# Linear attention ahead of two mixture layers: the exponentials of a chunk one step later in a hand-written pipeline

## Chip, cores and metric

The kernel runs on one core of a Trainium2 chip. The metric is device time in microseconds (us), the median of several runs. The engines are named as the profile names them: PE (TensorE, its matmuls), PEld (its weight loads), DVE (VectorE), ACT (ScalarE), POOL (GpSimd) and SP (SyncE, which here only issues transfers). Each engine runs its own instructions strictly in program order.

## What is computed

Three parts follow each other: attention with random features, a gated layer and a layer that mixes eight experts. Only the first is touched.

```python
def phi(x):                      # x: q or k, scaled by 64 ** -0.25
    proj = einsum('bhsd,md->bhsm', x, omega)
    h = proj - sum(x * x, -1) / 2
    return exp(h - max(h, -1)) / sqrt(m)
kv  = einsum('bhsm,bhsd->bhmd', phi(k), v);  z = sum(phi(k), 2)
out = (phi(q) @ kv) / (phi(q) @ z + 1e-6)    # batch 4, heads 8, 576 positions, width 64, 128 features
x = moe2(moe(out))
```

## The kernel before

The attention cuts q and k into 36 chunks of 128 partitions by 512 numbers (eight groups of 64). Chunk 0 and chunk 17 hold the tails of k, 18 and 35 those of q; the rest alternate, k on odd and q on even numbers. A pipeline that is written out by hand goes through them in steps. The list ORDER (L63) says which stage is issued in which place of a step, and for which chunk: a pair (name, n) works on chunk step - n. So the order of the list is the order of each engine's queue, and n is how many steps after its own number a chunk reaches a stage. The stages are:

- load and loadv (L442, L453), on SP's queue: x two steps ahead, v one step ahead, ahead of all else in the step.
- s0 (L467): squares of x on POOL into one buffer, and two foldings there, from 64 to 16 per group (chunk 0 takes the square on ACT and is not folded). s0r (L482) sums them on DVE, s0n (L487) scales the sums on POOL.
- s2p (L494): the projection, 16 small matmuls on PE into one of two double banks of PSUM. s2m (L511): maximum of it on DVE. s2b and s2c (L515, L521): the bias of the exponentials, two small DVE operations. s2x (L525): the exponentials, 8 on ACT, four each in two places.
- s3 (L531): for k the product with v into a bank of the ring "nu" (banks 1 and 2), for q transposes into the ring of banks 0 and 3. s3a (L552): ACT copies them out.
- s4 (L565): for q the product with kv, in two halves into the two banks of "nu". s4d, s4r, s4n (L581 to L600): the denominators, their reciprocals and the quotient on DVE. s5 (L602): transposes of that, into banks 0 and 3. s5a on ACT and s5b on DVE (L618, L623): the result as a rounded part xh and a rest xl.
- pump (L629): one piece of work on the weights of the next layer (conversions on ACT, DVE and POOL).

Chunk i is projected in step i + 1. After 38 steps the first matmuls of the next layer (moe1, next(m1) at L662) are issued between the last stages, and the rings change to banks that these leave free (DRAIN, L646).

In a step of before, DVE's queue is in this order: s5b, s2m, s0r, s2b, s4d, s2c, the rest of s4, pump. ACT's is s5a, s3a, s2x, pump, with one pump between the halves of s2x. So xl of a step stands ahead of its maximum, and the exponentials belong to the chunk whose maximum was taken in the same step.

Of the kernel before, what the change touches and what calls it, by code (L numbers as in the profile page):

```python
# [11 lines left out]
F32 = mybir.dt.float32  # L12
F32R = mybir.dt.float32r
AF = mybir.ActivationFunctionType
ALU = mybir.AluOpType
AX = mybir.AxisListType
# [4 lines left out]
P = 128  # L21
B, H, S, D = 4, 8, 576, 64
# [12 lines left out]
SCALE = float(D) ** -0.25  # L35
# [15 lines left out]
class Kernel:  # L51
    def __init__(self, tc, x, v, vt, omega, wg, wv, wo, w2g, w1, w2, out):
# [7 lines left out]

    ORDER = [("s5a", 7), ("s3a0", 4), ("s2p", 1), ("s5b", 7), ("s2m", 1), ("s40", 5), ("s0r", 0), ("s3a1", 4),  # L63
             ("s2b", 1), ("s4d0", 5), ("s2c", 1), ("s0", -1), ("s30", 3), ("s31", 3), ("s2x0", 1), ("s41", 5),
             ("s0n", 0), ("pump", 3), ("s5", 6), ("s2x1", 1), ("s4d1", 5), ("s4r", 5), ("s4n0", 5), ("s4n1", 5),
             ("pump", 4)]
    RINGS = dict(tr3=(0, 3), tr5=(0, 3), nu=(1, 2), a=(0, 1, 2, 3), b=(4, 5, 6, 7))

    DRAIN = dict(RINGS, tr3=(4, 5), tr5=(6, 4, 5), nu=(7, 6))


    EARLY = 1

# [322 lines left out]
    def attention(self, m1):  # L398
        tc, nc = self.tc, self.nc
        if True:  # L400
            af, ident = self.af, self.ident
            t0 = af.tile([P, 4, 512], F32, tag="t0", name="at0")
            t1 = af.tile([P, 2, 1024], F32, tag="t1", name="at1")
            t2 = af.tile([P, 4, 512], F32, tag="t2", name="at2")
# [3 lines left out]
            sm = af  # L408
# [27 lines left out]
            NCH = len(chunks)  # L436
# [5 lines left out]
            def load(i):  # L442
                side, bp, hp, j = chunks[i]
                c = st[i]
                n = 8 if hp is None else 2 * hp + j
                k = turn("x", 3)
                xt = c["xt"] = xts[turn("xt", 4)]
                c["x"] = t0[:, k].rearrange("p (a d) -> p a d", d=D)
                for w, t in ((0, t0[:, k]), (1, xt)):
                    nc.sync.dma_start(t, self.x["qk".index(side), w, bp, n])  # L450
                c["idx"] = (lambda a, h: 2 * a + h) if hp is None else (lambda a, h: 4 * h + a)

            def loadv(i):  # L453
                side, bp, hp, j = chunks[i]
                c = st[i]
                if side == "q":
                    return
                if hp is None:
                    c["vz"] = vzts[2 * bp:2 * bp + 2]
                    for j in range(2):  # L460
                        nc.sync.dma_start(c["vz"][j].rearrange("p a d -> p (a d)"), self.vt[bp, j])
                else:
                    z = c["vz"] = vz[nvz[0] % NVZ]
                    nvz[0] += 1
                    nc.sync.dma_start(z.rearrange("p a d -> p (a d)"), self.v[bp, 2 * hp + j])

            def s0(i):  # L467
                c = st[i]
                sqv = c["x"]
                if i < self.EARLY:  # L470
                    c["xx"] = t2[:, i].rearrange("p (a d) -> p a d", d=D)
                    c["ssq"] = sm.tile([P, 8], F32, tag="ssq", name=f"ssq{i}", bufs=4)
                    nc.scalar.activation(c["xx"], sqv, AF.Square)
                    return
                xx = t0[:, 3].rearrange("p (a d) -> p a d", d=D)
                nc.gpsimd.tensor_tensor(xx, sqv, sqv, op=ALU.mult)
                ssq = sm.tile([P, 8], F32, tag="ssq", name=f"ssq{i}", bufs=4)
                nc.gpsimd.tensor_tensor(xx[:, :, 0:32], xx[:, :, 0:32], xx[:, :, 32:64], op=ALU.add)
                nc.gpsimd.tensor_tensor(xx[:, :, 0:16], xx[:, :, 0:16], xx[:, :, 16:32], op=ALU.add)
                c["xx"], c["ssq"] = xx, ssq  # L480

            def s0r(i):  # L482
                c = st[i]
                xx = c["xx"] if i < self.EARLY else c["xx"][:, :, 0:16]
                nc.vector.tensor_reduce(c["ssq"], xx, axis=AX.X, op=ALU.add)

            def s0n(i):  # L487
                c = st[i]
                nsq = sm.tile([P, 8], F32, tag="nsq", name=f"nsq{i}", bufs=4)
                eng = nc.vector if i < self.EARLY else nc.gpsimd  # L490
                eng.tensor_scalar(nsq, c["ssq"], -SCALE * SCALE / 2, None, op0=ALU.mult)
                c["nsq"] = nsq

            def s2p(i):  # L494
                side, bp, hp, j = chunks[i]
# [132 lines left out]

            pump = lambda i: self.attn_pump()  # L629
            fns = dict(s0=s0, s0r=s0r, s0n=s0n, s2p=s2p, s2m=s2m, s2b=s2b, s2c=s2c, s4r=s4r, s5=s5, s5a=s5a, s5b=s5b, pump=pump)  # L630
            halves = dict(s2x=s2x, s3=s3, s3a=s3a, s4=s4, s4d=s4d, s4n=s4n)

            def stage(n):
                if n in fns:
                    return fns[n]
                g, h = halves[n[:-1]], int(n[-1])
                return lambda i: g(i, h)

            order = [(stage(n), k) for n, k in self.ORDER]
            nc.sync.dma_start(om2, self.omega)  # L640
            load(0)
            load(1)
            s0(0)
            for step in range(NCH + 7):
                if step == NCH + 2:
                    self.rings = self.DRAIN  # L646
                    self.upper.close()
                    psum = self.upper.enter_context(tc.tile_pool(name="upper", bufs=1, space=PSUM))
                    self.banks += [psum.tile([P, 512], F32, tag=f"b{i}", name=f"bank{i}") for i in range(4, 8)]
                if step + 2 < NCH:  # L650
                    load(step + 2)
                if step == 0:
                    loadv(0)
                if step + 1 < NCH:
                    loadv(step + 1)
                for fn, n in order:
                    i = step - n
                    if 0 <= i < NCH:
                        fn(i)
                self.attn_hook(step)  # L660
                if step >= NCH + 2:
                    next(m1)  # L662
# [868 lines left out]
```

## Time and profile before

| | |
|---|---|
| median of three runs | 2124.3 us (2119.33 to 2132.07) |
| the profiled execution | 2124.37 us, its span 2122.6 us |
| PE busy over the span | 2069.0 us (97%) |
| DVE, ACT, POOL busy | 1377.6, 806.3, 1042.8 us |
| attention, first projection to last | 5.19 to 187.2 us |

A view by windows gives for each stretch the busy time of each engine, with the number of instructions, and the granted clock of PE (1.00 is 2.4 GHz, 0.50 is 1.2 GHz). A timeline lists instructions by start and duration; in square brackets stands for how long the engine sat idle before, and who ended that. The chain of waits follows the work that ended last backwards from the end of the stretch. Busy spans of PE overlap a little, since matmuls are pipelined: the distance from one start to the next is what a group costs.

### The profile page before, as it was taken

The page shows a single profiled execution, that of the slowest core. Times are in us where ns is not written, and L with a number is a line of the kernel's source. Part 1 is how long each engine was busy: PE and PEld are TensorE (multiplying, and loading weights), DVE is VectorE, ACT ScalarE, POOL GpSimd, SP SyncE. Part 2 cuts the span into 40 slices and gives each one's busy share as a digit, 9 for nine tenths or more (in the row PEclk, how much of TensorE's full clock was granted, in tenths as well). Part 3 has the DMA queues.
Part 4 walks back from the last instruction along what each step waited for, and adds up shares of the span by engine and source line. Part 5 has one row for each costly group of instructions (what it writes and reads, how often), then busy time and mean ns, then how long its engine had stood idle before and what let it go on. Part 6 is the DMA issues. An engine that isn't in the chain of part 4 may idle for free.

```text
span 2122.6 us, 32786 instructions
## 1 busy us (share of the span) xinstructions
PE 2069.0 (97%) x11980; PEld 1999.3 (94%) x11980; DVE 1377.6 (65%) x2247; ACT 806.3 (38%) x1805; POOL 1042.8 (49%) x1046
## 2 busy tenths in 40 slices
PE   7799999999999999999999999999999999999998
PEld 6788999999998899899898999999999999999998
DVE  6765678877765654454445566666687766666666
ACT  5555433333344353344343433233233423323332
POOL 5653666656633454554653444444354543444433
PEclk9969999999999999999999999999999999999999
DMA  6441556555523567658658787777877877878784
GB/s 221 156 131 56 169 170 188 186 172 164 185 77 136 194 230 271 228 209 301 237 210 315 253 262 263 259 253 250 308 260 252 280 260 262 263 258 247 257 271 154
DMA packets 238130, 467.78 MB, mean 220 GB/s; under 512 B 20272, under 2 KB 110096, under 8 KB 233872
## 3 DMA queue, kind: packets, MB, share of 16 engines
q1 hardware_dynamic: 237968, 465.68, 64.9%
q8 instruction: 95, 1.56, 0.3%
q14 instruction: 67, 0.55, 0.1%
HBM read 340.25 MB, written 125.35 MB: 219 GB/s over the span
## 4 chain that ended last, share of the span: by engine, by line
PE 90%; DVE 6%; ACT 2%; issue 1%; POOL 0%; DMA 0%; DVEq 0%; SPq 0%; ACTq 0%; POOLq 0%
PE bank L1056 12%; PE bank L1302 7%; PE bank L1303 7%; PE bank L1304 7%; PE pair L1393 7%; PE pair L1394 7%; PE pair L1395 7%; PE bank L702 5%; PE bank L700 5%; PE bank L701 5%; PE bank L997 3%; PE bank L999 3%; PE bank L998 3%; PE bank L732 2%; PE bank L734 2%; PE bank L733 2%
## 5 line engine op out<-in xcount | busy, mean ns | idle before, releaser
L1405 DVE TENSOR_TENSOR sums<-pair,sums 128x768 f32<-128x768 f32 x209 | 198.6, 951 | 44.3 <-PE pair L1395 44.3
L1302 PE MATMUL bank<-xh,ar 128*128 128x384 f32 x564 | 188.7, 335 | 2.4 <-ACT mt L1335 2.0
L1304 PE MATMUL bank<-xh,ar 128*128 128x384 f32 x564 | 188.4, 334 | 0.0
L1303 PE MATMUL bank<-xl,ar 128*128 128x384 f32 x564 | 188.4, 334 | 0.0
L1072 DVE SCALAR_TENSOR_TENSOR ac<-bank,mt,ac 128x512 f32<-128x512 f32 x84 | 63.1, 751 | 132.4 <-PE bank L1056 132.4
L1393 PE MATMUL pair<-xh,ar 128*128 128x384 f32 x344 | 115.0, 334 | 0.2 <-DVE sums L1405 0.2
L1395 PE MATMUL pair<-xh,ar 128*128 128x384 f32 x344 | 114.9, 334 | 0.0
L1394 PE MATMUL pair<-xl,ar 128*128 128x384 f32 x344 | 114.9, 334 | 0.0
L1302 PEld LDWEIGHTS bank<-xh,ar 128*128 128x128 f32 x564 | 105.9, 188 | 3.4 <-ACT mt L1335 2.7
L1303 PEld LDWEIGHTS bank<-xl,ar 128*128 128x128 f32 x564 | 105.9, 188 | 0.0
L1304 PEld LDWEIGHTS bank<-xh,ar 128*128 128x128 f32 x564 | 105.8, 188 | 0.0
L714 ACT CAST ar<-mt 128x384 fp32r<-128x384 f32 x72 | 37.0, 514 | 170.5 <-DVE mt L711 170.5
L700 PE MATMUL bank<-xh,ar 128*128 128x384 f32 x288 | 96.5, 335 | 0.0
L702 PE MATMUL bank<-xh,ar1b 128*128 128x384 f32 x288 | 96.2, 334 | 0.0
L702 PE MATMUL bank<-xh,ar 128*128 128x384 f32 x288 | 96.2, 334 | 0.0
L701 PE MATMUL bank<-xl,ar 128*128 128x384 f32 x288 | 96.2, 334 | 0.0
L700 PE MATMUL bank<-xh,ar1b 128*128 128x384 f32 x288 | 96.2, 334 | 0.0
L701 PE MATMUL bank<-xl,ar1b 128*128 128x384 f32 x288 | 96.2, 334 | 0.0
L997 PE MATMUL bank<-xh,ar 128*128 128x384 f32 x264 | 89.4, 339 | 3.2 <-DVE st L1031 2.5
L999 PE MATMUL bank<-xh,ar 128*128 128x384 f32 x264 | 88.7, 336 | 0.6 <-DVE ar L264 0.5
L998 PE MATMUL bank<-xl,ar 128*128 128x384 f32 x264 | 88.4, 335 | 0.0
L1056 PE MATMUL bank<-ar,xh 128*128 128x512 f32 x324 | 84.8, 394 | 0.0
(378 smaller groups left out, 6770.6 us busy)
## 6 DMA issues: line engine op xcount, KB each, us to landing
ar<-w2forms SPq DMA_DIRECT2D x144, 512.0 KB, 4.5
ar<-w1forms SPq DMA_DIRECT2D x141, 512.0 KB, 5.0
ar1b<-w1forms SPq DMA_DIRECT2D x62, 512.0 KB, 4.9
ar1b<-w2forms SPq DMA_DIRECT2D x61, 512.0 KB, 4.6
w2forms<-ar SPq DMA_DIRECT2D x224, 128.0 KB, 4.2
w1forms<-ar SPq DMA_DIRECT2D x22, 1280.0 KB, 6.8
sumsraw<-in_w_dram SPq DMA_DIRECT2D x32, 512.0 KB, 4.5
w2forms<-sumsraw SPq DMA_DIRECT2D x128, 128.0 KB, 2.6
```

The source lines that it names most:

```text
L700: nc.tensor.matmul(t, hi[:, c, fs], self.xh[:, c, cs], start=(c == 0), stop=False)
L701: nc.tensor.matmul(t, hi[:, c, fs], self.xl[:, c, cs], start=False, stop=False)
L702: nc.tensor.matmul(t, lo[:, c, fs], self.xh[:, c, cs], start=False, stop=(c == KC - 1))
L997: nc.tensor.matmul(g, ah[:, c, :], bh[:, c, :], start=(first and c == 0), stop=False, skip_group_check=not first)
L1056: nc.tensor.matmul(y, a, w[:, fi % 2, ds], start=(first and x == 0 and k == 0 and fi == fis[0]), stop=(last and x == 1 and fi == fis[-1]))
L1302: nc.tensor.matmul(g, w[:, 0, d], bh[:, d, :], start=bool(first and d == 0), stop=False, skip_group_check=not first)
L1303: nc.tensor.matmul(g, w[:, 0, d], bl[:, d, :], start=False, stop=False, skip_group_check=not first)
L1304: nc.tensor.matmul(g, w[:, 1, d], bh[:, d, :], start=False, stop=(d == 1), skip_group_check=not first)
L1393: nc.tensor.matmul(y, w[:, k, 0, ds], h, start=(k == 0), stop=False)
L1394: nc.tensor.matmul(y, w[:, k, 0, ds], l, start=False, stop=False)
L1395: nc.tensor.matmul(y, w[:, k, 1, ds], h, start=False, stop=(k == 1))
L1405: v.tensor_tensor(a[n], pair, a[n], op=ALU.add)
```

## The change

ORDER is written anew. s2m, s2b, s2c and s2x move from 1 to 2 steps after a chunk's number, and all stages behind them move by one, so that a chunk takes one step more and the loop has one step more (44 instead of 43). The two double banks of the projection, the four buffers of exponentials and the three of v stay. Within a step DVE's queue becomes s0r, s2m, s2b, s2c, s5b, s4d, s4r, s4n, pump; PE's becomes s4, s2p, s3, s5; ACT's becomes s5a, s3a, s2x, s0n, pump. Both pumps stand at the end. The squares are no longer folded on POOL, so that the DVE sum reads 512 columns instead of 128; their scaling goes from POOL to ACT; and chunk 0 is no exception any more.

```diff
-    ORDER = [("s5a", 7), ("s3a0", 4), ("s2p", 1), ("s5b", 7), ("s2m", 1), ("s40", 5), ("s0r", 0), ("s3a1", 4),
-             ("s2b", 1), ("s4d0", 5), ("s2c", 1), ("s0", -1), ("s30", 3), ("s31", 3), ("s2x0", 1), ("s41", 5),
-             ("s0n", 0), ("pump", 3), ("s5", 6), ("s2x1", 1), ("s4d1", 5), ("s4r", 5), ("s4n0", 5), ("s4n1", 5),
-             ("pump", 4)]
+    ORDER = [("s5a", 8), ("s3a0", 5), ("s3a1", 5), ("s0r", 0), ("s2m", 2), ("s2b", 2), ("s2c", 2), ("s0", -1),
+             ("s5b", 8), ("s40", 6), ("s41", 6), ("s2p", 1), ("s30", 4), ("s31", 4), ("s2x0", 2), ("s2x1", 2),
+             ("s0n", 0), ("s5", 7), ("s4d0", 6), ("s4d1", 6), ("s4r", 6), ("s4n0", 6), ("s4n1", 6), ("pump", 3), ("pump", 4)]
...
-    EARLY = 1
...
             def s0(i):
                 c = st[i]
-                sqv = c["x"]
-                if i < self.EARLY:
-                    c["xx"] = t2[:, i].rearrange("p (a d) -> p a d", d=D)
-                    c["ssq"] = sm.tile([P, 8], F32, tag="ssq", name=f"ssq{i}", bufs=4)
-                    nc.scalar.activation(c["xx"], sqv, AF.Square)
-                    return
-                xx = t0[:, 3].rearrange("p (a d) -> p a d", d=D)
-                nc.gpsimd.tensor_tensor(xx, sqv, sqv, op=ALU.mult)
-                ssq = sm.tile([P, 8], F32, tag="ssq", name=f"ssq{i}", bufs=4)
-                nc.gpsimd.tensor_tensor(xx[:, :, 0:32], xx[:, :, 0:32], xx[:, :, 32:64], op=ALU.add)
-                nc.gpsimd.tensor_tensor(xx[:, :, 0:16], xx[:, :, 0:16], xx[:, :, 16:32], op=ALU.add)
-                c["xx"], c["ssq"] = xx, ssq
+                x = c["x"]
+                xx = c["xx"] = t0[:, 3].rearrange("p (a d) -> p a d", d=D)
+                nc.gpsimd.tensor_tensor(xx, x, x, op=ALU.mult)
...
-                xx = c["xx"] if i < self.EARLY else c["xx"][:, :, 0:16]
-                nc.vector.tensor_reduce(c["ssq"], xx, axis=AX.X, op=ALU.add)
+                c["ssq"] = sm.tile([P, 8], F32, tag="ssq", name=f"ssq{i}", bufs=4)
+                nc.vector.tensor_reduce(c["ssq"], c["xx"], axis=AX.X, op=ALU.add)
...
-                nsq = sm.tile([P, 8], F32, tag="nsq", name=f"nsq{i}", bufs=4)
-                eng = nc.vector if i < self.EARLY else nc.gpsimd
-                eng.tensor_scalar(nsq, c["ssq"], -SCALE * SCALE / 2, None, op0=ALU.mult)
-                c["nsq"] = nsq
+                c["nsq"] = sm.tile([P, 8], F32, tag="nsq", name=f"nsq{i}", bufs=4)
+                nc.scalar.activation(c["nsq"], c["ssq"], AF.Copy, scale=-SCALE * SCALE / 2)
...
-            for step in range(NCH + 7):
+            for step in range(NCH + 8):
```

## Rows read from the trace of the kernel before

**Rows 1.** Windows; columns: stretch, length, busy (instructions) by engine, granted clock, DMA, GB/s

```profile
215.00:400.00 185.00, 185.00 (x1069) 185.00 (x1068) 141.94 (x204) 72.51 (x145) 113.61 (x110) 1.00 0.57 178
...
24.00:99.00 75.00, 59.86 (x582) 53.76 (x581) 57.54 (x119) 46.96 (x154) 48.62 (x68) 0.98 0.49 163
99.00:116.00 17.00, 17.00 (x99) 15.38 (x97) 10.53 (x20) 9.35 (x31) 11.48 (x15) 0.50 0.27 84
...
136.60:167.40 30.80, 30.80 (x171) 29.00 (x169) 17.65 (x38) 14.96 (x50) 14.80 (x23) 0.50 0.37 114
```

**Rows 2.** Timeline of PE, projections (s2p) alone; columns: start, duration, engine, line, operation

```profile
21.43 2.08 PE L509 MATMUL two<-om,turned 64*128 64x128 f32 x16
24.73 1.16 PE L509 MATMUL two<-om,turned 64*128 64x128 f32 x16
...
99.31 2.08 PE L509 MATMUL two<-om,turned 64*128 64x128 f32 x16
...
114.10 2.08 PE L509 MATMUL two<-om,turned 64*128 64x128 f32 x16
...
138.82 2.08 PE L509 MATMUL two<-om,turned 64*128 64x128 f32 x16
...
167.69 1.16 PE L509 MATMUL two<-om,turned 64*128 64x128 f32 x16
...
186.03 1.16 PE L509 MATMUL two<-om,turned 64*128 64x128 f32 x16
```

**Rows 3.** Chain of waits, 50 to 73 us; columns: start, duration, work

```profile
52.77 1.13 DVE mx L513
...
55.16 0.42 DVE m1raw L205
...
55.91 0.75 DVE at L600 x2
...
59.49 2.18 ACT turned L529 x8
61.66 0.48 ACT xh L621
...
62.17 0.69 DVE xl L626
62.87 1.13 DVE mx L513
```

**Rows 4.** Timeline, 52 to 84 us, PE over one k and one q chunk

```profile
56.39 1.11 PE L544 MATMUL bank<-at,at 128*128 128x66 f32 x8 [0.98 <-DVE at L600]
...
59.21 1.16 PE L509 MATMUL two<-om,turned 64*128 64x128 f32 x16
...
60.30 1.11 PE L578 MATMUL bank<-at,at 128*128 128x66 f32 x8
...
62.92 0.66 PE L549 MATMUL bank<-ident,at 128*128 128x128 f32 x4 [1.07 <-DVE xl L626]
...
64.35 1.16 PE L509 MATMUL two<-om,turned 64*128 64x128 f32 x16
```

**Rows 5.** Timelines, DVE and POOL: a bias beside a square, one alone, one sum unfolded

```profile
64.27 1.04 POOL L476 TENSOR_TENSOR at<-at 128x512 f32<-128x512 f32 x1 [0.90 <-DVE hm L519]
64.30 1.03 DVE L523 SCALAR_TENSOR_TENSOR bi<-hm,nsq 128x8 f32<-128x8 f32 x1
...
185.98 0.18 DVE L523 SCALAR_TENSOR_TENSOR bi<-hm,nsq 128x8 f32<-128x8 f32 x1
...
4.52 0.69 DVE L485 TENSOR_REDUCE ssq<-at 128x8 f32<-128x512 f32 x1 [4.52 <-ACT at L473]
```

**Rows 6.** Timeline of PE: first matmuls after its idle time, ahead of the two slow stretches

```profile
98.66 0.72 PE L610 MATMUL bank<-ident,at 128*128 128x128 f32 x4 [2.65 <-ACT at L562]
...
136.39 0.89 PE L549 MATMUL bank<-ident,turned 128*128 128x128 f32 x4 [1.43 <-DVE xl L626]
```

**Rows 7.** Groups by line, 24 to 187 us; columns: operation, count, busy us, mean ns, idle

```profile
L523 DVE SCALAR_TENSOR_TENSOR bi<-hm,nsq 128x8 f32<-128x8 f32 x31 | 29.4, 949 | 0.9 <-DVE den L590 0.2
```

## Prediction

> **What bounds the kernel now.** I read the windows first. Behind the attention PE is busy in all 185.00 of 185.00 us at clock 1.00 [rows 1]: nothing in the diff touches that part, so whatever the attention gives up or gains moves the end by as much. Between 24 and 99 us PE is busy in only 59.86 of 75.00 us, and DVE in 57.54, ACT in 46.96 [rows 1]: no engine is full, so a chain through several engines sets the pace. In two stretches the granted clock is 0.50, the 1.2 GHz level, and PE is full in both, 17.00 of 17.00 and 30.80 of 30.80 us [rows 1]: there PE itself is the bound.
>
> The starts of the projections give the pace, one for each step. From 24.73 to 186.03 us there are 30 steps in 161.30 us [rows 2]. At the low clock two take 114.10 - 99.31 = 14.79 and four take 167.69 - 138.82 = 28.87, so 6 steps in 43.66, 7.28 each. The other 24 take 117.64 us, 4.90 each.
>
> The chain of waits says what makes 4.90 [rows 3]. Exponentials 2.18, then xh 0.48 behind them in ACT's queue, then xl 0.69 on DVE, and only behind it in DVE's queue the next maximum, 1.13, on which the bias and the next exponentials wait. Two maxima behind an xl, at 52.77 and 62.87 us, lie 10.1 us, two steps, apart [rows 3]. PE has less to do than that. From 56.39 to 64.35 us it does a k product, two halves of a q product, the transposes and one projection, with 1.07 us of idle in between; a second projection costs 60.30 - 59.21 = 1.09 [rows 4]. So its own pair of steps is 7.96 - 1.07 + 1.09 = 7.98 us, 3.99 a step.
>
> **What the change does, part by part.** The profiled execution took 2124.37 us, practically the median of 2124.3, and the sum is made against it.
>
> The move of the exponentials. Maximum and bias of a step now read a projection of the step before and stand ahead of xl. The path from the exponentials over xh and xl to the next maximum is cut. What is late next? I follow the new queues. ACT's step begins with s5a and s3a, which wait for PE's last matmuls of the step before; the exponentials come behind them. The second half of a q product needs the bank of "nu" that the k product of the step before filled, so it waits until ACT has copied that out, behind the exponentials of the step before. This closes a loop once in two steps: second half of the q product 1.11 [rows 4]; on DVE a conversion, denominators and reciprocal 55.91 - 55.16 = 0.75, quotient 0.75 [rows 3]; sum of squares 0.69 [rows 5], maximum 1.13 [rows 3], two bias operations at 0.18 [rows 5]; exponentials 2.18 [rows 3]; the scaling on ACT, one eighth of that at most, 0.27; xh 0.48 and the k copy, which is smaller, 0.48 at most [rows 3]. That is 8.20, with four hand-overs of about 0.05 (61.66 + 0.48 to 62.17 is 0.03, 62.17 + 0.69 to 62.87 is 0.01) 8.4. PE's own 7.98 lies under it. Conversions on ACT and collisions with POOL come on top now and then: I take 8.6, 4.3 a step, an estimate from these rows. The ends are 3.99, PE's own, and 4.7, below.
>
> So the 24 steps gain 24 x (4.90 - 4.3) = 14.4 us.
>
> The clock. Both slow stretches began after PE had sat idle: 2.65 us up to 98.66 and 1.43 us up to 136.39 [rows 6]. Those waits were for ACT and xl, the path that is cut; in the new loop PE waits about 8.6 - 7.98 = 0.6 us in two steps. I take it that the clock stays up in the steady part. Then 6 x 7.28 = 43.66 becomes 6 x 4.3 = 25.8, a gain of 17.9. The bounds are 0 and 17.9.
>
> The squares. The foldings leave POOL, which waits for DVE before every square (0.90 us in this row [rows 5]); nothing on the path waits for POOL's adds, so this is worth nothing directly. The DVE sum reads 512 columns, 0.69 instead of a folded one; it is in the loop above. It stands first in DVE's step and waits for a POOL square that was issued a step earlier: one step of cover. If the cover is gone, the square's 1.04 [rows 5] is paid in that step.
>
> The bias beside the square. With a square on POOL a bias takes 1.03 and both end together at about 65.3 us; without one it takes 0.18 [rows 5], and the mean of 31 is 0.949 [rows 7]. The new square is released by the sum of squares, ahead of the maximum, so its 1.04 runs under the 1.13 of the maximum and the bias should be short. The price for the other case is a rival below. The Trainium skill (SBUF — State Buffer, section "SBUF: two separate sides") says that a DVE operation with two SBUF inputs and a GpSimd operation take an exclusive pair of ports, the second waiting until the first has ended. The rows agree: 64.30 + 1.03 is the end of the square, within 0.02. By that rule the sum is the one below where the square is over before the maximum ends, and that of the second rival where a square or a conversion on POOL still lies beside the bias.
>
> Queues. SP: the load of a v now waits for a k product one step later, and the x loads queue behind it; an x of 256 KB takes 1.6 us at the 163 GB/s of the first stretch [rows 1], and it is needed a step later by POOL and three steps later by PE. Covered by a step of 4.3; uncovered it would cost up to 1.6 a step. ACT: the scaling waits for a sum that stands first in DVE's step, so nothing queues behind it.
>
> The ends of the pipeline. One step more: a last chunk's transposes and product move behind the projections, where the next layer's matmuls fill PE. I take 1 us; bounds 0 and 3.99. The beginning: PE runs at the low clock's pace up to 24.73 (2.08 for a projection at 21.43, 1.16 at 24.73 [rows 2]). Now its first steps hold projections alone, since the products come a step later, so I expect it to come up later. I take two steps at 7.28 instead of 4.3, 6.0 us; bounds 0 and 30.8, the longest slow stretch seen, 4.2 steps or 12.6 us.
>
> Sum: 2124.4 - 14.4 - 17.9 + 1 + 6 = 2099.1 us.
>
> **The rivals.**
>
> *The clock drops as before.* PE still waits on a bank in every pair of steps, in short stretches. Against it: the two drops above followed idle times of 1.43 and 2.65 us. With six slow steps left, where PE is full and the move is worth nothing: 2124.4 - 14.4 + 7 = 2117. The Trainium skill (TensorE: Matmul & The Clock Gate, section "A second HAM failure mode: psum-queue depth-cycling") tells of a kernel whose many short waits between groups of matmuls kept the gate going up and down. By that rule this rival would hold; the rows here show drops after longer waits.
>
> *The bias stays long.* If squares or conversions on POOL still cover it, the loop has 0.949 for 0.18: 8.6 + 0.77 = 9.4, 4.7 a step. For: 31 biases with a mean of 0.949 [rows 7]. Gain 24 x 0.20 + 43.66 - 28.2 = 20.3, so 2124.4 - 20.3 + 7 = 2111.
>
> *PE stays cold.* Slower than before: with projections alone at the beginning PE does not come up, and each step at 7.28 costs 2.98 more than one at 4.3. With n slow steps the change is -32.3 + 1 + 2.98 n; it is nought at n = 10.5 and +0.5% at n = 14. At n = 17 it is 2144. For: in 30.80 us of full PE the clock did not rise [rows 1]. Against: that is four steps, not ten.
>
> *It doesn't do what it says.* The pair is held at 10.1 us by something that I don't see, PE's order for example, and all stays as it is: 2124 or, with the longer ends, 2131.
>
> **How the numbers follow.** Forecast 0.56, clock drops as before 0.19, bias long 0.15, cold 0.06, no effect 0.04. The forecast's case alone spans 2088 (no cold steps at the beginning and 4.15 a step) to 2106. The range goes up to 2117, through the bias case and half of the clock case, and leaves out about 0.2. About 0.5% (10.6 us) is what a measurement of this kernel can tell from no change, so faster means under 2113.7: all of the forecast, two thirds of the bias case, a third of the clock case, 0.56 + 0.10 + 0.06 = 0.72. Slower by over 0.5% is the cold case with a little of the last, 0.07; the rest, 0.21, is no change.
>
> **What would show it.** The chain of waits in a steady stretch should no longer go from xl to the maximum. Projections at clock 1.00 should start 4.3 us apart, the bias should take about 0.18 us, xl should still wait for xh without holding anyone, and PE's idle times should be near 0.6 us, before the second half of a q product and ended by the copy on ACT. The windows from 24.73 us on should show clock 1.00 but for the beginning. I am wrong if the granted clock falls again in the middle of the attention, if the steps at full clock stay above 4.7, or if the time from the last projection to the next layer grows by more than a step.

## The result and the profile after

The changed kernel takes 2101.64 us, the median of four runs (2101.5 to 2103.08), against 2124.95 beside it: a ratio of 0.989, with a 95% interval of 0.986 to 0.992. The forecast was 2099.1, faster. The profiled execution took 2101.5 us, its span 2099.7, which is 22.9 less than the 2122.6 of before.

Of the page's busy times POOL lost 52.5 us, PE 15.0 (2069.0 to 2054.0) and DVE 1.6, and ACT gained 4.9.

```profile
PE 2054.0 (98%) x11980; PEld 1986.8 (95%) x11980; DVE 1376.0 (66%) x2246; ACT 811.2 (39%) x1840; POOL 990.3 (47%) x942
```

Windows (columns as in [rows 1]): from just before the rise of the clock to the last projection, and the same later stretch as before.

```profile
28.40:161.75 133.35, 124.09 (x1177) 113.66 (x1176) 108.34 (x228) 97.97 (x336) 45.51 (x42) 0.92 0.52 166
...
215.00:400.00 185.00, 185.00 (x1069) 185.00 (x1068) 143.29 (x210) 67.95 (x135) 115.37 (x111) 1.00 0.57 181
```

The layers behind the attention are as full as before [rows 1], so the gain lies in the attention, where PE is now busy in 93% of the time and the granted clock is 0.92. It isn't 1.00 yet.

The projections on PE (they are now line 495) give the pace, as in [rows 2]. The sixth is the first row.

```profile
26.13 2.08 PE L495 MATMUL two<-om,turned 64*128 64x128 f32 x16
29.47 1.16 PE L495 MATMUL two<-om,turned 64*128 64x128 f32 x16
...
56.10 1.16 PE L495 MATMUL two<-om,turned 64*128 64x128 f32 x16
61.97 1.16 PE L495 MATMUL two<-om,turned 64*128 64x128 f32 x16
64.09 1.16 PE L495 MATMUL two<-om,turned 64*128 64x128 f32 x16
...
161.75 1.16 PE L495 MATMUL two<-om,turned 64*128 64x128 f32 x16
```

The same 30 steps as before take 161.75 - 26.13 = 135.62 us instead of 161.30, 4.52 each. They begin 26.13 - 24.73 = 1.40 us later, and from the last projection to the end it takes 2099.7 - 161.75 = 1937.95 us instead of 2122.6 - 186.03 = 1936.57. So the 22.9 us are 25.68 less in the steps, 1.40 more ahead of them and 1.38 more behind.

What lies behind is not all the pipeline's end. The same matmul of the next layer, the 10300th of PE's matmul records counted from the end, starts at 243.00 us before (line 702) and at 221.87 after (line 688). From the last projection to it, called the drain below, it takes 56.97 us before and 60.12 after, 3.15 more. From it to the end it takes 1879.60 and 1877.83 us, although the change touches nothing there.

The steps are uneven. The pair from 56.10 to 64.09 takes 7.99 us, PE's own 7.98 [rows 4]; every second or third pair takes 9.6 to 11.3 (from 44.83 to 56.10 us, for example). A timeline of such a pair, four engines:

```profile
46.81 1.27 POOL L177 TENSOR_TENSOR ar<-cv,ar 128x512 fp32r<-128x512 f32 x1
...
46.90 1.20 DVE L505 SCALAR_TENSOR_TENSOR hm<-mx,nsq 128x8 f32<-128x8 f32 x1
...
48.40 2.18 ACT L515 ACTIVATE at<-two,bi 128x128 f32<-128x128 f32 x8 [2.77 <-DVE bi L509]
...
50.72 1.28 POOL L209 TENSOR_TENSOR cv<-cv,m1raw 128x512 f32<-128x512 f32 x1
50.82 1.21 DVE L509 SCALAR_TENSOR_TENSOR bi<-hm,nsq 128x8 f32<-128x8 f32 x1
50.98 0.35 ACT L544 ACTIVATE at<-bank 128x132 f32<-128x132 f32 x1
51.38 1.11 PE L564 MATMUL bank<-at,at 128*128 128x66 f32 x8 [1.73 <-ACT at L544]
...
52.42 1.85 PE L495 MATMUL two<-om,turned 64*128 64x128 f32 x16
```

Read it from the top. A conversion of weights on POOL (L177) lies beside the first bias operation, which takes 1.20 us instead of 0.17 and ends with it (46.90 + 1.20 = 48.10, 46.81 + 1.27 = 48.08). ACT waits 2.77 us for the bias, the exponentials end late, the scaling, xh and the copy of the k product (L544) stand behind them, and PE's second half of the q product waits 1.73 us for the bank that this copy frees. Then the projection takes 1.85 us instead of 1.16: the clock has fallen to 1.2 GHz. Five such falls come between the sixth projection and the last, after PE waits of 1.73, 1.28, 2.25, 0.97 and 1.73 us. Four of these waits are for that copy; the one of 2.25 is a projection's, for exponentials. A wait of 0.95 us had no fall behind it (the projection takes 1.16 us), the one of 0.97 had:

```profile
69.86 1.11 PE L564 MATMUL bank<-at,at 128*128 128x66 f32 x8 [0.95 <-ACT at L544]
70.90 1.16 PE L495 MATMUL two<-om,turned 64*128 64x128 f32 x16
...
115.92 1.11 PE L564 MATMUL bank<-at,at 128*128 128x66 f32 x8 [0.97 <-ACT at L544]
116.96 1.57 PE L495 MATMUL two<-om,turned 64*128 64x128 f32 x16
```

The chain of waits, 50 to 73 us, shows one step of the new order (columns as in [rows 3]):

```profile
64.14 0.59 DVE ssq L473
64.73 1.14 DVE mx L499
...
65.89 0.18 DVE hm L505
...
66.10 0.18 DVE bi L509
...
66.36 2.18 ACT at L515 x8
68.54 0.10 ACT nsq L478
```

No xl stands ahead of the maximum any more, and in this step the bias is 0.18. In the mean it is 0.405 instead of 0.949 [rows 7]; the group by line, DVE, from 28.4 to 161.75 us:

```profile
L509 DVE SCALAR_TENSOR_TENSOR bi<-hm,nsq 128x8 f32<-128x8 f32 x30 | 12.2, 405 | 1.0
```

### The profile page after: what moved, and what is told of

It is laid out like the page before. It is cut to its first block, busy times and chain, and to the rows that moved or that the text cites. A ratio compares the mean times of both kernels' runs of the same rounds, so it can differ in the third digit from the quotient of the medians.

```text
span 2099.7 us, 32728 instructions
## 1 busy us (share of the span) xinstructions
PE 2054.0 (98%) x11980; PEld 1986.8 (95%) x11980; DVE 1376.0 (66%) x2246; ACT 811.2 (39%) x1840; POOL 990.3 (47%) x942
## 4 chain that ended last, share of the span: by engine, by line
PE 92%; DVE 4%; ACT 2%; issue 1%; DMA 0%; POOL 0%; SPq 0%; DVEq 0%; ACTq 0%; POOLq 0%
PE bank L1042 13%; PE bank L1288 7%; PE bank L1289 7%; PE bank L1290 7%; PE pair L1379 7%; PE pair L1380 7%; PE pair L1381 7%; PE bank L686 5%; PE bank L687 5%; PE bank L688 5%; PE bank L983 4%; PE bank L985 4%; PE bank L984 3%; PE bank L718 2%; PE bank L720 2%; PE bank L719 2%
```

## Experiments

The kernel before takes 2114 to 2133 us from run to run, the others vary less; differences under about 5 us between two experiments are not told apart by their times alone, so each is read by its steps as well. Each experiment was run beside its own runs of before (medians of 2124.95 to 2130.86 us), and the ratio goes by those. "Thirty steps" are those from the sixth projection to the last, in the one execution that was profiled; "the rest" is from the last projection to the end, and "the drain" is the first part of that. What lies behind the drain, the same code in every row, takes 1876.7 to 1881.1 us, so a difference of up to some 4 us between two rests needs no cause in the pipeline.

| kernel | median us (runs) | ratio to before | thirty steps | the rest | the drain |
|---|---|---|---|---|---|
| before | 2124.95 | 1 | 161.3 | 1936.6 | 57.0 |
| the change | 2101.64 (4) | 0.989 (0.986 to 0.992) | 135.6 | 1938.0 | 60.1 |
| offsets only | 2155.24 (4) | 1.0148 (1.0117 to 1.018) | 182.1 | 1943.3 | 62.5 |
| order only | 2102.35 (4) | 0.9897 (0.9869 to 0.9925) | 137.9 | 1937.7 | 57.6 |
| squares only | 2121.45 (10) | 0.9991 (0.997 to 1.0013) | 156.7 | 1941.5 | 60.4 |
| folded squares | 2096.2 (4) | 0.9872 (0.9845 to 0.9899) | 125.9 | 1940.5 | 60.2 |
| order, folded squares | 2095.17 (4) | 0.9835 (0.9815 to 0.9854) | 135.5 | 1932.6 | 55.9 |
| scaling on POOL | 2093.41 (4) | 0.983 (0.9809 to 0.9851) | 124.6 | 1940.4 | 60.2 |
| no conversions | 2122.58 (1) | | 118.5 | | |
| late half | 2113.49 (5) | 0.9925 (0.9901 to 0.995) | 143.5 | 1940.4 | 62.2 |
| next layer later | 2103.89 (4) | 0.9901 (0.9871 to 0.993) | 136.3 | 1935.0 | 56.7 |
| early matmuls | 2102.29 (4) | 0.9899 (0.9865 to 0.9933) | 135.3 | 1938.0 | 60.1 |
| conversions behind bias | 2095.82 (4) | 0.9871 (0.9841 to 0.9902) | 131.1 | 1940.0 | 61.6 |
| scaling on POOL, next layer later | 2088.51 (5) | 0.9826 (0.9797 to 0.9854) | 124.2 | 1933.6 | 56.8 |

### Lag or order

The change moves four stages by one step and writes a new order. First the lag without the order, in the kernel before:

```diff
-    ORDER = [("s5a", 7), ("s3a0", 4), ("s2p", 1), ("s5b", 7), ("s2m", 1), ("s40", 5), ...
+    ORDER = [("s5a", 8), ("s3a0", 5), ("s2p", 1), ("s5b", 8), ("s2m", 2), ("s40", 6), ...
```

> The kernel before with the offsets of the change (maximum, bias, exponentials and all stages behind them one step later, 44 steps) and nothing else: the order within a step and the squares stay. Theory A: what held the steps at 4.90 us was the order of DVE's queue (xl ahead of the maximum, xl behind xh, xh behind the exponentials of the step before), and one step of lag does not cut it. Then the time is that of before: 2119 to 2130 us, projections 4.8 to 5.1 us apart at full clock. Rival B, the lag itself lets the engines overlap: at most 2108 us.

It takes 2155.24 us, which neither theory had: not the same, but 1.5% slower. The windows show a clock of 0.78 in its thirty steps, and the chain of waits why:

```profile
28.64:212.00 183.36, 151.90 (x1194) 140.84 (x1194) 102.22 (x225) 95.49 (x309) 92.71 (x132) 0.78 0.40 123
```

```profile
85.59 1.05 ACT at L529 x4
...
86.69 2.08 PE two L509 x16
88.77 1.92 PE bank L578 x8
...
90.71 0.16 DVE den L590
90.87 0.25 DVE bi L523
...
91.20 0.37 ACT at L529 x2
```

The projection waits for the exponentials of the step before. A projection needs the double bank of the chunk two before it, and with the lag the exponentials of that chunk run one step later, in the step just before: the lag spends the step that the second bank had given. Behind the projection PE does the q product, its denominator stands ahead of the last bias operation in the old order, and the exponentials wait for that. So 17 of the thirty projections behind the sixth wait for ACT, 0.50 to 4.37 us, a new loop closes in each step with a q product, and xl still stands ahead of the maximum besides.

Then the order without the lag, in the changed kernel:

```diff
-    ORDER = [("s5a", 8), ("s3a0", 5), ("s3a1", 5), ("s0r", 0), ("s2m", 2), ("s2b", 2), ("s2c", 2), ...
+    ORDER = [("s5a", 7), ("s3a0", 4), ("s3a1", 4), ("s2p", 1), ("s0r", 0), ("s2m", 1), ("s2b", 1), ("s2c", 1), ...
```

> The new order within a step and the new squares, but the offsets of before: maximum and exponentials belong to the projection of the same step, which is put first in PE's step; 43 steps. Theory A, the order cuts the path: the maximum waits 1.1 us for its projection, but no more for xl, so most of the gain is kept: 2100 to 2108 us. Rival B, the lag is what counts: 2115 us or more.

2102.35 us: the whole gain, within what can be told apart. What counts is the order within a step, here still with the new squares. With the squares of before on top of the same edit (their diff stands below, under folded squares):

> The new order within a step with the offsets and the squares of before (projection first in PE's step, 43 steps, squares folded and scaled on POOL). Theory A: the order alone is the gain; the lag of one step adds nothing and takes the free step of the projection's double bank; the unfolded squares cost time through the clock. Then 2093 to 2099 us, as with the lag and folded squares (2096.2). Rival B, the lag is worth something once the squares are folded: 2101 us or more.

2095.17 us, against 2096.2 with lag and folded squares. Theory A holds for the total, and the order alone, with neither the lag nor the new squares, is faster than before by 1.65%. Which of its entries counts (xl behind the bias, both pumps at the end, PE's order) was not tried one by one; for xl speaks the chain, where it stood in the path before [rows 3] and is gone after.

Where the theory says that the lag adds nothing, the parts speak against it. With the lag thirty steps take 125.9 us instead of 135.5. It loses 2.2 us at the start (the sixth projection comes at 28.21 instead of 26.00 us) and 4.3 in the drain (60.2 and 55.9); another 3.6 are lost behind the drain, where both kernels are the same. So this run does not show that the lag is worth nothing, only that its gain in the steps did not reach the total.

### The squares

The squares' part alone, in the kernel before (new s0, s0r and s0n, and the sum first):

```diff
-    ORDER = [("s5a", 7), ("s3a0", 4), ("s2p", 1), ("s5b", 7), ("s2m", 1), ("s40", 5), ("s0r", 0), ...
+    ORDER = [("s0r", 0), ("s5a", 7), ("s3a0", 4), ("s2p", 1), ("s5b", 7), ("s2m", 1), ("s40", 5), ...
```

> The kernel before with the squares' part alone: no folding on POOL, the scaling on ACT, the sum of squares first in DVE's step; offsets and the rest of the order as before, xl still ahead of the maximum. Theory A, the path through DVE has two parts that can be shortened on their own: a bias that waits for the square on POOL (1.03 for 0.18 us) and a sum that stands between maximum and bias (0.2 us). Taken from 10.1 us in two steps, 2 x 0.8 and 2 x 0.2 less give some 8.2 to 8.5: 2102 to 2112 us. Rival B, only the place of xl counts and the squares are worth nothing: 2119 to 2128 us.

2121.45 us, no change that can be measured, so my theory A fell. Thirty steps are 4.6 us shorter than before, the drain 3.4 us longer. Its mechanism is there, but only while the clock is up:

```profile
26.00:80.00 54.00, 46.47 (x462) 42.27 (x459) 40.51 (x89) 37.61 (x132) 21.70 (x20) 1.00 0.58 173
...
24.00:181.60 157.60, 140.32 (x1197) 127.98 (x1195) 105.57 (x236) 100.57 (x349) 49.85 (x46) 0.84 0.48 145
```

Ten steps from 28.47 to 73.88 us take 4.54 each (before, ten from 28.44 to 78.85 take 5.04), and then the clock falls (a mean of 0.58 from 80 to 92 us, with PE busy in 12.00 of 12.00). Over the whole stretch it is 0.84, as before.

The other way round, the changed kernel with the squares of before (s0, s0r and s0n as they were, the order stays):

```diff
-                nc.gpsimd.tensor_tensor(xx, x, x, op=ALU.mult)
+                nc.gpsimd.tensor_tensor(xx, sqv, sqv, op=ALU.mult)
+                nc.gpsimd.tensor_tensor(xx[:, :, 0:32], xx[:, :, 0:32], xx[:, :, 32:64], op=ALU.add)
+                nc.gpsimd.tensor_tensor(xx[:, :, 0:16], xx[:, :, 0:16], xx[:, :, 16:32], op=ALU.add)
...
-                nc.scalar.activation(c["nsq"], c["ssq"], AF.Copy, scale=-SCALE * SCALE / 2)
+                eng.tensor_scalar(nsq, c["ssq"], -SCALE * SCALE / 2, None, op0=ALU.mult)
```

> The changed kernel with the squares as before (folded twice on POOL, scaled on POOL, sum of 128 columns on DVE), the sum still first in a step. Theory A: the square and its foldings (1.04 + 0.80 + 0.46 us) start behind the sum and reach past the maximum (1.13 us), so that bias operations wait about 1.1 us for POOL in each step, which takes back some of the gain: 2106 to 2116 us and a mean bias of over 0.7 us. Rival B, the squares don't count and the sum is 0.4 us shorter: 2097 to 2102 us.

2096.2 us: faster than the change, although the bias has a mean of 0.597 us in it. Its time is a little under rival B's range, and theory A's long bias doesn't decide.

```profile
L521 DVE SCALAR_TENSOR_TENSOR bi<-hm,nsq 128x8 f32<-128x8 f32 x32 | 19.1, 597 | 1.3
```

Which part of the squares costs? One edit of the changed kernel:

```diff
-                nc.scalar.activation(c["nsq"], c["ssq"], AF.Copy, scale=-SCALE * SCALE / 2)
+                nc.gpsimd.tensor_scalar(c["nsq"], c["ssq"], -SCALE * SCALE / 2, None, op0=ALU.mult)
```

> The changed kernel with one edit: the scaling of the sums goes back from ACT (0.26 us in each step) to POOL; no folding. It asks which of the squares' costs lengthens the loop. Theory A, the scaling on ACT, ahead of the copies that PE waits for: 2095 to 2099 us, close to folded squares. Rival B, the longer sum on DVE (0.68 for 0.28 us) or when conversions on POOL meet the bias: 2100 to 2103 us, as the change.

2093.41 us, so of the squares' parts it is the scaling that costs: 0.26 us on ACT in each step, ahead of the copies that PE waits for. The intervals of the two ratios, 0.983 and 0.989, don't overlap. With the scaling on POOL the mean of the bias also falls, to 0.241, as the groups by line show (24 to 160 us), and the clock is 0.97 over thirty steps. How much of the 8 us is ACT's own time and how much is fewer meetings on POOL stays open; that folded squares, also scaled on POOL, take nearly the same thirty steps (125.9 and 124.6 us) with a bias of 0.597 speaks for ACT.

```profile
L509 DVE SCALAR_TENSOR_TENSOR bi<-hm,nsq 128x8 f32<-128x8 f32 x32 | 7.7, 241 | 1.3
```

```profile
28.00:152.57 124.57, 119.82 (x1193) 110.06 (x1192) 102.12 (x228) 96.52 (x314) 54.73 (x73) 0.97 0.57 182
```

### What still holds PE

The conversions out of the steps:

```diff
-             ("s0n", 0), ("s5", 7), ..., ("s4n1", 6), ("pump", 3), ("pump", 4)]
+             ("s0n", 0), ("s5", 7), ..., ("s4n1", 6)]
...
                 self.attn_hook(step)
+                if step == NCH + 2:
+                    self.flush()
```

> The changed kernel without the two pieces of weight conversion in each step; all of them run in one go ahead of the next layer, so that the end of the attention shows a gap of 20 to 30 us and the total means nothing. Theory A, a conversion on POOL that holds a bias, or one on ACT ahead of the copies, makes the long waits of PE (up to 1.73 us) after which the clock falls: without them two steps take 8.0 us throughout, no wait of PE is over 0.7 us, the granted clock stays at 1.00 from its first rise to the last projection, and 30 steps take 120 to 124 us instead of 135.6. Rival B, the waits come from the loop itself: pairs of steps of over 10 us and falls of the clock remain.

```profile
28.50:146.00 117.50, 116.39 (x1192) 107.10 (x1192) 88.03 (x207) 93.35 (x330) 28.06 (x27) 1.00 0.48 154
```

```profile
104.96 1.16 PE L495 MATMUL two<-om,turned 64*128 64x128 f32 x16
107.08 1.16 PE L495 MATMUL two<-om,turned 64*128 64x128 f32 x16
112.95 1.16 PE L495 MATMUL two<-om,turned 64*128 64x128 f32 x16
```

Theory A, to the letter: pairs of 7.99 us (104.96 to 112.95), PE busy in 116.39 of 117.50 us, no wait over 0.46 us, clock 1.00 throughout. Thirty steps take 118.5 us. So in the changed kernel the conversions, with the falls of the clock that follow, cost 135.6 - 118.5 = 17.1 us. Their work has to be done somewhere, so that isn't all to be had.

Can the wait be covered? The projection between the two halves of the q product:

```diff
-             ("s5b", 8), ("s40", 6), ("s41", 6), ("s2p", 1), ("s30", 4), ...
+             ("s5b", 8), ("s40", 6), ("s2p", 1), ("s41", 6), ("s30", 4), ...
```

> The changed kernel with one edit: on PE the projection stands between the two halves of the q product instead of behind both, so that 1.1 us of other work lies ahead of the half that waits for the bank of the k product. Theory A, that wait is what still holds PE: waits ahead of it fall to 0.7 us at most, the clock falls less often, 2094 to 2099 us. Rival B, the projection then waits for the exponentials of the step before, or the falls of the clock have another cause: 2100 to 2105 us.

2113.49 us, slower than the change by 12 and beyond rival B's range, by the mechanism of rival B: PE now waits ahead of the projection, up to 4.38 us, for the exponentials of the step before.

```profile
98.10 2.08 PE L496 MATMUL two<-om,turned 64*128 64x128 f32 x16 [4.38 <-ACT at L516]
```

And the conversions in another place, with the scaling on POOL:

```diff
-             ..., ("s2c", 2), ("s0", -1), ("s5b", 8), ..., ("s4n1", 6), ("pump", 3), ("pump", 4)]
+             ..., ("s2c", 2), ("s0", -1), ("pump", 3), ("pump", 4), ("s5b", 8), ..., ("s4n1", 6)]
```

> The changed kernel with the scaling on POOL and both pieces of weight conversion moved from the end of a step to behind the bias: on DVE they then lie behind the bias, on ACT ahead of the exponentials (where ACT waits for the bias in every second step), on POOL behind the square. Theory A, conversions cost because of their place in the loop: pairs of steps near 8.0 us, 30 steps in 120 to 124 us, 2086 to 2092 us. Rival B, ahead of the exponentials they delay those instead, or hold the next bias just as well: 2093 us or more.

2095.82 us, no better than the 2093.41 without the move, so theory A's 2086 to 2092 is missed, as rival B has it. In the profiled execution thirty steps take 131.1 us instead of 124.6, and the projection twice waits for exponentials (1.19 and 1.01 us); but that execution, with 2101.89 us, was the slowest of the four, the others took 2094.72 to 2096.48. That a conversion ahead of the exponentials costs as much as one at the end of a step fits the totals; where it is paid in a usual execution is not shown.

### The ends of the pipeline

The term for a late rise of the clock:

```diff
                     if 0 <= i < NCH:
                         fn(i)
+                for _ in range({0: 20, 2: 20, 3: 6, 4: 3}.get(step, 0)):
+                    nc.tensor.matmul(self.banks[3][:, 0:P], ident, ident, start=True, stop=True)
```

> The changed kernel with matmuls on the identity added, whose result nobody reads: 20 in step 0, 20 in step 2, 6 and 3 in the next two, where PE waits. It measures the term of the sum for a late rise of the clock (6.0 us). Theory A, the first steps run at 1.2 GHz because PE idles between projections; with the added work the clock rises some 10 us earlier and the steps up to the sixth projection, bound by PE from 19.65 us on, come 3 to 6 us sooner: 2096 to 2099 us. Rival B, the added work only delays the projections or the clock falls again: 2101 to 2105 us.

The clock rises earlier (a projection takes 1.16 us from the third on), and the time stays, 2102.29 us. The sixth projection comes at 25.36 us instead of 26.13, only 0.77 sooner, because it then waits for the exponentials:

```profile
15.40 1.16 PE L495 MATMUL two<-om,turned 64*128 64x128 f32 x16
...
25.36 1.16 PE L495 MATMUL two<-om,turned 64*128 64x128 f32 x16 [1.20 <-ACT turned L515]
```

So in this run the low clock at the beginning is nearly free. The run is no clean measure of it: the added matmuls themselves hold PE, and the fifth projection comes at 20.62 us instead of 19.65. From the fifth to the sixth it takes 4.74 us instead of 6.48, so 1.74 us come back there, against the 6.0 of the forecast.

The drain, with the next layer a step later:

```diff
-                if step >= NCH + 2:
+                if step >= NCH + 3:
                     next(m1)
```

> The changed kernel with one edit: the next layer's first matmuls are issued from step 39 on instead of 38, so that they keep the place that they had before relative to the last chunk. From the last projection to the end the changed kernel takes 2099.7 - 161.75 = 1937.95 us, before 2122.6 - 186.03 = 1936.6, and PE waits 2.14 us there for xl, behind the next layer's work on ACT. Theory A, the longer drain is paid there: the rest after the last projection falls to 1932 to 1936 us, the total to 2097 to 2100. Rival B, the later start leaves PE idle for as much as is gained: 2101 to 2105 us.

The rest falls to 1935.0 us, as theory A has it, and PE's wait of 2.14 us for xl is gone. The drain is 3.4 us shorter (56.7 instead of 60.1). The total of 2103.89 is not told apart from 2101.64, so this alone is inconclusive. In the changed kernel that wait reads:

```profile
178.35 1.40 PE L564 MATMUL bank<-at,at 128*128 128x66 f32 x8 [2.14 <-DVE xl L612]
```

The edit of the scaling and this one together, both diffs as above:

> Two edits of the changed kernel together: the scaling of the sums on POOL (alone 2093.4 us) and the next layer's first matmuls one step later (alone the rest after the last projection fell from 1937.95 to 1935.0 us). Theory A, the two lie in different places and add up: 30 steps in about 125 us as with the first, 1935 us behind the last projection instead of 1940.4, so 2087 to 2092 us. Rival B, a PE that has less to do in step 38 gives back in front of the next layer what the drain gains: 2092 to 2097 us.

2088.51 us (2087.2 to 2092.28), with 124.2 us for thirty steps and 56.8 for the drain instead of 60.2: both parts are there. The rest falls by 6.8 us, to 1933.6, but only 3.4 of that lie in the drain. It is the fastest that was run, 13 us under the change; by the ratio, 0.9826, it is not told apart from the scaling alone (0.983) or from the order with folded squares and no lag (0.9835). It has the lag without the longer drain; the same kernel without the lag was not run.

## Why the prediction was right

**The bound.** Right. The layers behind are untouched, and by the chain of waits the path from xl to the maximum was what held the steps. The experiments make it sharper: the new order alone brings the gain; the move to the next step, on which the prediction built ("maximum and bias of a step now read a projection of the step before"), gains nothing in the total and by itself loses 1.5%.

**The pace.** I had 4.3 us a step at full clock, from a loop of 8.4 us over the bank of "nu", with 8.6 taken. The wait is where I put it, ended by the copy on ACT, but only in the pairs that a conversion disturbs. The size was averaged wrongly: in quiet pairs the loop is under PE's own 7.98, and where a conversion meets a bias the pair takes 9.6 to 11.3 us. In the forecast's terms thirty steps were 126 us for the loop (8.4 a pair) and 3 for conversions and collisions (0.2 a pair); measured are 118.5 without conversions and 17.1 for them, with the falls of the clock that follow. Two errors in opposite ways, 7.5 and 14.1 us, leave 6.6.

**The clock.** I took it to stay up. It fell five times, shortly: its mean over the steps is 0.92, against 0.84 over 24 to 187 us before. The prediction named a new fall in the middle of the attention as a sign that it was wrong, and in this step it was. Gains of 14.4 and 17.9, 32.3 in all, stand against 25.7 measured. The rival "the clock drops as before" came true in part, by the mechanism it named, PE's waits on a bank. In the run without conversions the waits and the falls are gone together. The ground for the step was also too narrow: it held the two waits of [rows 6] against the rival, but the kernel before has a short fall whose last wait ahead of it is 0.99 us, among the 24 steps that were counted at full clock, and a wait of 1.81 us with none behind it:

```profile
45.67 1.11 PE L544 MATMUL bank<-at,turned 128*128 128x66 f32 x8 [0.99 <-DVE at L600]
...
48.97 2.08 PE L509 MATMUL two<-om,turned 64*128 64x128 f32 x16
...
93.42 0.66 PE L549 MATMUL bank<-ident,turned 128*128 128x128 f32 x4 [1.81 <-DVE xl L626]
...
94.85 1.16 PE L509 MATMUL two<-om,turned 64*128 64x128 f32 x16
```

The Trainium skill (TensorE: Matmul & The Clock Gate, section "A second HAM failure mode: psum-queue depth-cycling") tells of a kernel whose PE idled so often for short times between groups of matmuls that the gate went up and down. The five falls after waits of 0.97 to 2.25 us agree with that; that waits of up to 1.55 us passed without one in the run with folded squares shows that such waits alone don't bring it about.

**The bias.** Forecast 0.18, measured 0.405 in the mean. The square did move out of its way; conversions on POOL did not. The Trainium skill (SBUF — State Buffer, section "SBUF: two separate sides") says that of a DVE operation with two SBUF inputs and a GpSimd operation that reads SBUF the one that starts second waits until the first has ended. The rows at 46.81 and 46.90 agree within 0.02 us. The rival with 0.949 in every step and 2111 us did not come true.

**The squares.** I had them at nothing beyond the loop, and wrote that nothing queues behind the scaling on ACT. That step failed: the copies of the next step queue behind it, and with the scaling back on POOL the kernel takes 8 us less (2093.41 against 2101.64).

**The beginning.** Forecast 6.0 us for two more slow steps; measured 1.40. The clock did rise later, between the projections at 26.13 and 29.47 us. But the third to the fifth projection wait for exponentials, and with early matmuls the sixth does too, so that little of the low clock reaches the total.

**The drain.** Forecast 1, with bounds of 0 and 3.99. From the last projection to the end 1.38 us more are measured, but 3.15 up to the same matmul of the next layer; the other 1.77 came back behind that, where the kernels are the same. The lag is what lengthens it: without it, with the new squares, the drain is 57.6 us.

So the sum came out near, -25.3 forecast and -22.9 measured in the profiled execution, and that is in part luck: the steps were forecast with 6.6 us too much gain, the beginning with 4.6 too much loss, and inside the steps two larger errors cancelled.

## What to carry to other kernels

In engines that run in program order, look first at what stands ahead of the operation on the path in its own queue; a new order there was worth 1.0% with the new squares, while one more step of lag used up the free step of a double buffer and was worth nothing in the total. Price a moved operation in the queue that receives it, by what queues behind it: with 0.26 us in each step on ACT the kernel took 8 us more here. Where a side job comes every few steps, don't spread it over a mean step: find the step that it hits, and what the clock does after it.

## What the runs showed of the hardware that was not expected

A low clock is not always a cost: with 49 more matmuls (98 in the profile) ahead of the steady part PE had come up to 2.4 GHz by the third projection, and the kernel took the same time. And falls of the clock followed waits as short as 0.97 us in the changed kernel and 0.82 in the order with folded squares, while with lag and folded squares waits of up to 1.55 us passed without a fall: from 31.58 us to the last all projections take 1.16 us. No run here separates what decides. Two rows of the order with folded squares, then two of lag and folded squares:

```profile
76.64 1.11 PE L577 MATMUL bank<-at,at 128*128 128x66 f32 x8 [0.82 <-ACT at L557]
...
79.36 2.08 PE L508 MATMUL two<-om,turned 64*128 64x128 f32 x16
```

```profile
103.64 0.69 PE L574 MATMUL bank<-at,at 128*64 128x66 f32 x16 [1.55 <-ACT at L556]
104.25 1.16 PE L507 MATMUL two<-om,turned 64*128 64x128 f32 x16
```

The granted clock has a gap at the start of a trace: it can read 1.00 while the matmuls still run at the lower level. In folded squares it is 1.00 from 24 us on, although the projection at 28.21 us takes 2.08. For the first steps the durations of the projections are the safer reading.
